# Output products of a fused attention and expert kernel: one-bank PSUM tiles instead of two-bank tiles, and a list maker that counts a matmul's restart

## The chip, the cores and the metric

One NeuronCore of one Trainium2 chip runs the whole program. The metric is device time in microseconds of one execution; lower is better. Before the change the median of three runs is 1176.81 us (1176.42 to 1177.85).

## The reference

An attention block with pooled keys feeds two feed-forward blocks. All arithmetic is float32.

```python
a = softmax(phi, axis=2)                              # per head, 576 tokens x 32 memories
k_m, v_m = a^T k, a^T v
x = softmax(q k_m^T / 8) v_m                          # -> x: 2304 tokens x 512
h = x @ w_in; x = (h * cos(h)) @ w_out                # 512 -> 2048 -> 512
p = domain_probs / (domain_probs.sum(-1) + 1e-9)      # 2304 x 4
for e in range(4):
    out += p[:, e:e+1] * (max(x @ w1[e], 0) @ w2[e])  # 512 -> 1024 -> 512 for each expert
```

## The kernel before, in words

A float32 product is made of three passes (`mm3`, L308): each operand is split into a high and a low float32r part, and high times high, high times low and low times high are added up in PSUM.

**Two stages.** The attention and the first feed-forward block end at about 377 us; they follow a written order (`PLAN`) and the change does not touch them. The second stage, the four experts, is the rest. It runs over u (two halves of the tokens), s (16 slices of 256 hidden columns, four for each expert) and j (two token groups of a half, 512 and 640 tokens). One (u, s, j) is a unit; there are 64.

**A unit** has these parts. `hidden` (L1060, task H) makes x @ w1 with seven block products in place of eight (a Strassen-like scheme), each of six matmuls, of 256 or of 320 columns, in three PSUM banks out of a ring `p` of four. Between some products ScalarE copies a partial sum out (tiles `p1`, `u2`, `u3`, names p and u in the trace), and VectorE adds them (L925, tile `c`); so the chain of a unit goes back and forth between engines. `rectify` (L1122, task R) applies the maximum with zero.

In the **first half** (u = 0), `plain_out` (L1184, task O) multiplies a tile of 128 tokens with w2: six matmuls of 512 columns fill one PSUM bank, and VectorE's `gather` (L934) scales by p and adds to `acc` (L939; L937 where s = 0, the first write). A unit has four or five such tiles, a slice nine. They are grouped in twos: a task takes one entry of the ring `po`, that is a PSUM tile `op` of two banks, and makes product, gather, product, gather in it (L1193 to L1206). There are two such entries, so four banks. The group with the fifth tile uses one of its two banks.

In the **second half** (u = 1) the output is made for pairs of token tiles by the same seven-product scheme: `pair_prep` (L1214) builds the operands and `pair_out` (L1266) makes seven products of three matmuls with 256 columns each, in one two-bank tile `op` of the ring `po`. Names in the code: px is in the first bank, pz and py share the second. px is used over and over: m1, out, m6, out, m7, out, m4, out. The first "out" (e1) goes over ScalarE (tile `ev`, L341) with an addition afterwards, the next ones (e3, e5) over VectorE's gather. Then e6 gathers px and py together (512 columns), m3 adds to py, and e7 gathers pz and py (512 columns). The tokens that are left over in a half take `plain_out` with a bank of the ring `p`.

**The order of the work** is made while the program is built, by the class `Order` (L148). Each task is a generator that yields one operation after the other; its next operation is its head. `run` (L225) looks at all heads, reckons for each when it could start (`start`, L191: when its engine is free and its dependencies have ended, by the planned durations), and puts the earliest one into the program, between equals the one with the lower rank. Ranks: H of unit i has 10 i, O of unit i has 10 i + 11 and up (u = 0) or 10 i + 13 and up (u = 1). The engines then run their lists in order. Waits between engines come from the tile framework, by what each instruction reads and writes of a tile.

```python
t = max([self.at[eng], *(d.end for d in op.deps)])            # L192
o = yield pe(1400, 130, mm, t0, done[key], done["wb", u, s])  # L1204
m1 = yield prod(px, 0, 0, t0, ...)                            # L1304
m2 = yield prod(pz, 1, 1)
e1 = yield from grown(0, da[:, 0], op[:, px], pa, m1)
m5 = yield prod(py, 3, 3)
m6 = yield prod(px, 4, 4, e1, more=True)
```

Of the kernel before, what the change touches and what calls it, by code (L numbers as in the profile page):

```python
# [9 lines left out]
F32 = mybir.dt.float32  # L10
# [7 lines left out]
PSUM = bass.MemoryType.PSUM  # L18
# [47 lines left out]
class Have:  # L66
    def __init__(self, keys):
# [64 lines left out]
FIRST = "00 01 10 11 02 12 03 13".split()  # L132
PAIRS = ((0,), (1,), (2, 3), (4, 5), (6, 7))
RINGS = dict(phi=3, kv=4, q=4, raw=2, wi=2, wf=1, wo=2, es=2, st=2, stT=1, kvs=1, vw=2, y=2, kk=1, gt=3, h=2, o=2, c=2,
             p2=2, raw2=2, tt=1, wa=2, wb=2, wt=2, cq=2, p1=1, u2=1, u3=1, ht=2, h7=4, h1=1, sm=2, p=4, po=2, ev=4)
PATIENCE = {"PE": 0.0, "ACT": 0.5, "DVE": 0.5, "POOL": 1.0, "SP": 0.5, "X": 0.0}
RK = (0, -2, 8, 13, 20)
EV, ONE_P = (0,), True
RX = (12, 305, 333)
BW, BP, BX, RL = 20.0, 1.5, 1.2, -15  # L140
HOP = 90.0
TABLE_NS = 1283.0
DMA_NS = 1.0 / 370.0
DMA_LAG = 2000.0
# [3 lines left out]
class Order:  # L148
# [3 lines left out]
    def __init__(self):  # L152
        self.at = dict.fromkeys(("PE", "ACT", "DVE", "POOL", "SP", "X"), 0.0)
        self.table, self.port, self.bus = None, 0.0, 0.0
        self.tasks = {}
        self.done = {}
        self.left = {}
        self.log = []

    def add(self, name, rank, gen):  # L160
        self.tasks[name] = [rank, gen, None, name]
# [26 lines left out]
            else:  # L188
                return

    def start(self, op, eng):  # L191
        t = max([self.at[eng], *(d.end for d in op.deps)])  # L192
        if eng == "ACT" and op.table and op.table != self.table:
            t += TABLE_NS
        return max(t, self.port) if eng in op.port else t
# [29 lines left out]
    def run(self):  # L225
        while self.tasks:
            moved = None
            while moved != (moved := [t[2] for t in self.tasks.values()]):
                for task in sorted(self.tasks.values(), key=lambda t: t[0]):
                    self.poll(task)  # L230
            heads = []
            for task in self.tasks.values():
                if isinstance(task[2], Op):
                    op = task[2]
                    engs = op.engs if op.free else op.engs[:1]
                    _, t, eng = min((self.start(op, e) + op.ns[e] * (op.free if e == "DVE" and op.free else 1.0), self.start(op, e), e)
                                    for e in engs)
# [9 lines left out]
def tile_kernel(  # L247
# [17 lines left out]
    NT, DM = out.shape  # L265
# [68 lines left out]
    def have(*keys):  # L334
        return Have(keys)
# [10 lines left out]
    def pe(ns, lat, fn, *deps, fill=None):  # L346
        return Op("PE", ns, fn, *deps, lat=lat, fill=fill)
# [560 lines left out]
    dram = ctx.enter_context(tc.tile_pool(name="dram", bufs=1, space=bass.MemoryType.DRAM))  # L908
    p_ctx.close()
    ps_p = ctx.enter_context(tc.tile_pool(name="ps_p", bufs=4, space=PSUM, reuse_waits="tile"))  # L910
    ps_q = ctx.enter_context(tc.tile_pool(name="ps_q", bufs=2, space=PSUM, reuse_waits="tile"))

    PROD = {1: (0, 0), 2: (1, 1), 3: (2, 2), 4: (6, 3), 5: (3, 4), 6: (4, 5), 7: (5, 6)}
    HD2 = DM // 2
# [42 lines left out]
        todo.count((kind, 0, s), USERS[kind], R[kind], k, o)  # L957

    NBYTES = {"wa": 128 * 4 * 2 * XOPS * 256, "wb": 128 * 4 * 2 * NFC * DM, "wt": 128 * 4 * 8 * HD2}
    USERS = {"wa": 3, "wb": 6, "wt": 1}  # L960

    def make_wa(s):
        yield have(("wa?", s - 1), ("wb?", s - 1))
# [217 lines left out]
        n = seq.setdefault(name, len(seq))  # L1181
        return ("O?", n - 1), ("O?", n)

    def plain_out(i, tts, name, at, key, free):  # L1184

        u, s, j = units[i]
        before_, mine = turn(name)
        yield have(key, ("wb", u, s), before_, ("x", 0, 1))
        ring = "p" if u and ONE_P else "po"
        ko, t0 = yield R[ring]  # L1190
        todo.set(mine, None)
        wb, kb_ = w[u * NS2 + s][1]
        if ring == "po":  # L1193
            op = ps_q.tile([128, 2, DM], F32, tag="q", name="op")
        else:
            op = ps_p.tile([128, 1, DM], F32, tag="p", name="op")
        for e, tt in enumerate(tts):
            lt = at(tt)

            def mm():  # L1200
                for fc in range(NFC):
                    mm3(op[:, e], lambda x: lt(x, fc), lambda x: wb[:, x, fc, :], fc == 0, fc == NFC - 1)

            o = yield pe(1400, 130, mm, t0, done[key], done["wb", u, s])  # L1204
            ti, p_ = share(i, tt)
            g = yield gather(DM, outv[:, ti, :], op[:, e], p_, s == 0, o, done["x", 0, 1])  # L1206
            if d := store(i, ti, g):
                yield d
        R[ring].give(ko, g)
        free(o)  # L1210
        todo.set(("done", name), None)
        todo.count(("wb", u, s), USERS["wb"] - u, R["wb"], kb_, o)

    def pair_prep(i, k):  # L1214

# [50 lines left out]
    def pair_out(i, k, name):  # L1266

        u, s, j = units[i]
        before_, mine = turn(name)
        yield have(("h7", i, k), ("wb", u, s), ("wt", u, s), before_, ("x", 0, 1))  # L1270
        ko, t0 = yield R["po"]
        todo.set(mine, None)
        (wb, kb_), (wt, kt) = w[u * NS2 + s][1:]
        ht, kh = h7s[i, k]
        b = [lambda x: wb[:, x, 0, :HD2], lambda x: wb[:, x, 1, :HD2], lambda x: wb[:, x, 1, HD2:]]
        b += [lambda x, m=m: wt[:, x, m] for m in range(4)]
        op = ps_q.tile([128, 4, HD2], F32, tag="q", name="op")
        px, pz, py = 0, 2, 3
        (ia, pa), (ib, pb) = (share(i, t) for t in tiles_of(j)[0][k])
        da, db = (outv[:, i_, :].rearrange("p (x d) -> p x d", x=2) for i_ in (ia, ib))  # L1280

        def prod(at, oa, ob, *deps, more=False):
            return pe(357, 130, lambda: mm3(op[:, at], lambda x: ht[x][:, oa], b[ob], not more, True, True), *deps)

        first = s == 0

# [14 lines left out]
        def plus(dst, t, o, kt):  # L1301
            R["ev"].give(kt, (yield two_(HD2, dst, dst, t, o, op=ALU.add)))

        m1 = yield prod(px, 0, 0, t0, done["h7", i, k], done["wb", u, s], done["wt", u, s])  # L1304
        m2 = yield prod(pz, 1, 1)
        e1 = yield from grown(0, da[:, 0], op[:, px], pa, m1)
        m5 = yield prod(py, 3, 3)
        m6 = yield prod(px, 4, 4, e1, more=True)
        e3 = yield from grown(1, da[:, 1], op[:, px], pa, m6)
        m7 = yield prod(px, 5, 5, e3, more=True)  # L1310
        e5 = yield from grown(2, db[:, 1], op[:, px], pb, m7)
        m4 = yield prod(px, 2, 6, e5, more=True)
        if first:
            e6 = yield gather(HD2, db[:, 0], op[:, px], pb, True, m4)
            e6 = yield gather(HD2, db[:, 1], op[:, py], pb, False, m5)
        else:
            e6 = yield gather(DM, db, op[:, px::py - px], pb, False, m4, m5)
        m3 = yield prod(py, 6, 2, e6, more=True)
        R["h7"].give(kh, m3)
        todo.count(("wb", u, s), USERS["wb"] - u, R["wb"], kb_, m3)  # L1320
        todo.count(("wt", u, s), 4, R["wt"], kt, m3)
        if d := store(i, ib, e6):
            yield d
        e7 = yield gather(DM, da, op[:, pz:], pa, False, m3, m2)
        R["po"].give(ko, e7)
        if d := store(i, ia, e7):
            yield d

    def swap():
# [6 lines left out]
        todo.set("swap", None)  # L1336

    with tc.manual_schedule():
        for kind in ("wa", "wb", "wt"):
            todo.set(("got?", kind, -1), None)  # L1340
        todo.set(("wa?", 1), None)
# [15 lines left out]
        for i, (u, s, j) in enumerate(units):  # L1357
            todo.add(f"H{i}", 10 * i + RK[0], hidden(i))
            nt = 2 * SUBS[j][1] // 128
            if not u:  # L1360
                groups = [list(range(t, min(t + 2, nt))) for t in range(0, nt, 2)]
                for g, tts in enumerate(groups):
                    def free(o, i=i, n_=len(groups)):
                        todo.count(("ht", i), n_, R["ht"], cs_[i][1], o)
# [3 lines left out]
                    todo.add(f"O{i}.{g}", 10 * i + 11 + g, plain_out(i, tts, f"O{i}.{g}", at, ("ht", i), free))  # L1368
                todo.add(f"R{i}", 10 * i + RK[1], rectify(i))
                continue  # L1370
            todo.add(f"R{i}", 10 * i + RK[1], rectify(i))
            def pairs(i=i):
                for k in range(2):
                    todo.add(f"P{i}.{k}", 10 * i + RK[2] + k, pair_prep(i, k))
                    todo.add(f"O{i}.{k}", 10 * i + RK[3] + k, pair_out(i, k, f"O{i}.{k}"))

            def left(i=i, j=j):
                todo.add(f"Q{i}", 10 * i + RK[2] + 2 * (i != FINAL), one_prep(i))
                for t in tiles_of(j)[1]:
                    todo.add(f"O{i}.2", 10 * i + RK[3] + 2 * (i != FINAL), plain_out(  # L1380
                        i, [t], f"O{i}.2", lambda tt: lambda x, fc: ones_[i][0][:, x, fc], ("h1", i),
                        lambda o: R["h1"].give(ones_[i][1], o)))
            for f in (left, pairs) if i == FINAL else (pairs, left):
                f()
# [55 lines left out]
```

## Time and profile before

| | |
|---|---|
| median of three runs | 1176.81 us |
| the profiled execution | 1176.0 us |
| its span, first to last instruction | 1174.2 us |
| TensorE busy (matmuls) | 1141.1 us, 97% |
| VectorE, ScalarE, GpSimd busy | 797.4, 547.6, 674.9 us |
| mean granted TensorE clock | 0.995 |

The matmuls' ends in the profile are modelled: two that follow each other overlap in their rows. So the engine's pace is read from the starts. A matmul row comes with a row of its weight load (PEld), which runs ahead under the matmul before it; where a matmul has to wait for a semaphore, its weight load waits too.

### The profile page before, as it was taken

What the parts mean: (1) busy time and instruction counts of PE and PEld (TensorE: products, weight loads), DVE (VectorE), ACT (ScalarE), POOL (GpSimd) and SP (SyncE); (2) the same over time, 40 slices, a digit from 0 to 9 for tenths busy, and PEclk for the clock granted to TensorE, in tenths of its full rate; (3) what the DMA queues carried; (4) which work ended last, traced back from release to release, by engine and by line L of the source; (5) the groups of instructions that cost most, each with busy time, mean ns of one, the idle gap of its engine ahead of it and who ended that gap; (6) DMA issues with size and microseconds to landing.
All of it is one profiled execution on the core that took longest, in us unless ns stands there. A gap on an engine that the chain in (4) does not pass through costs nothing.

```text
span 1174.2 us, 21445 instructions
## 1 busy us (share of the span) xinstructions
PE 1141.1 (97%) x8432; PEld 1053.5 (90%) x8432; DVE 797.4 (68%) x1328; ACT 547.6 (47%) x1113; POOL 674.9 (57%) x964
## 2 busy tenths in 40 slices
PE   8999999999999899999999999999999999999997
PEld 7689999999999788888888888888999999999996
DVE  5888778788777655555555555687676767676766
ACT  4886555455544333343333333344554454545552
POOL 1555243133214458667776677756777676766764
PEclk9999999999999999999999999999999999999999
DMA  8931212211103444655666556692643454335412
GB/s 301 369 94 43 86 55 73 75 53 37 37 1 144 162 152 177 254 189 189 239 256 251 195 188 224 268 363 103 242 163 135 158 199 183 135 136 222 182 73 81
DMA packets 46485, 190.43 MB, mean 162 GB/s; under 512 B 6192, under 2 KB 15408, under 8 KB 34096
## 3 DMA queue, kind: packets, MB, share of 16 engines
q1 hardware_dynamic: 46384, 189.06, 43.7%
q8 instruction: 66, 1.08, 0.4%
q14 instruction: 35, 0.29, 0.1%
HBM read 121.41 MB, written 67.63 MB: 161 GB/s over the span
## 4 chain that ended last, share of the span: by engine, by line
PE 89%; DVE 6%; DMA 2%; ACT 1%; issue 1%; SPq 0%; DVEq 0%; ACTq 0%
PE op L310 49%; PE hp L310 36%; DVE acc L939 2%; DMA q<-in_qt_dram 1%; PE vw_ps L594 1%; DVE h L355 1%; PE warm L724 1%; DMA kv<-in_kv_dram 1%; PE sc L531 1%; ACT ev L341 1%; DVE x L355 1%; PE kvp L478 0%; SPq L338 0%; DVE c L925 0%; DVE sA L355 0%
## 5 line engine op out<-in xcount | busy, mean ns | idle before, releaser
L310 PE MATMUL hp<-x,wa 128*128 128x320 f32 (+1 forms) x2688 | 406.9, 296 | 6.0 <-DVE c L925 3.5
L310 PEld LDWEIGHTS hp<-x,wa 128*128 128x128 f32 x2688 | 379.1, 188 | 19.6 <-DVE c L925 5.2
L939 DVE SCALAR_TENSOR_TENSOR acc<-op,p_all,acc 128x512 f32<-128x512 f32 (+1 forms) x402 | 260.5, 662 | 184.0 <-PE op L310 180.2
L310 PE MATMUL op<-wb,ht 128*128 128x512 f32 x864 | 225.1, 402 | 5.7 <-DVE acc L937 4.0
L310 PE MATMUL op<-gt,wo 128*128 128x288 f32 x1536 | 218.9, 296 | 0.7 <-DVE acc L698 0.6
L310 PEld LDWEIGHTS op<-gt,wo 128*128 128x128 f32 x1536 | 208.2, 188 | 6.6 <-issue 2.8
L310 PEld LDWEIGHTS op<-wb,ht 128*128 128x128 f32 x864 | 156.3, 189 | 43.1 <-DVE acc L939 9.6
L355 POOL TENSOR_TENSOR gt<-y,gt 128x576 fp32r<-128x576 f32 x41 | 60.4, 1472 | 165.3 <-ACT gt L341 142.8
L341 ACT ACTIVATE u<-hp 128x320 f32<-128x320 f32 (+1 forms) x128 | 52.6, 411 | 203.1 <-PE hp L310 203.1
L310 PE MATMUL op<-wt,h 128*128 128x256 f32 x768 | 121.9, 286 | 9.5 <-ACT ev L341 5.8
L310 PEld LDWEIGHTS op<-wt,h 128*128 128x128 f32 x768 | 104.6, 189 | 15.2 <-ACT ev L341 8.7
L355 POOL TENSOR_TENSOR sm<-c 128x128 f32<-128x128 f32 x128 | 62.3, 491 | 92.5 <-ACT c L341 92.1
L310 PE MATMUL op<-wb,h 128*128 128x256 f32 (+1 forms) x672 | 113.1, 298 | 2.1 <-DVE acc L939 2.0
L310 PE MATMUL hp<-attnT,vw 128*128 128x288 f32 x768 | 112.4, 296 | 0.5 <-POOL attnT L355 0.5
L310 PEld LDWEIGHTS hp<-attnT,vw 128*128 128x128 f32 x768 | 105.1, 188 | 3.3 <-issue 1.2
L698 DVE TENSOR_TENSOR acc<-op,acc 128x576 f32<-128x576 f32 (+1 forms) x120 | 84.4, 710 | 32.4 <-PE op L310 31.6
L310 PEld LDWEIGHTS op<-wb,h 128*128 128x128 f32 x672 | 94.4, 189 | 5.7 <-DVE acc L939 2.1
L355 POOL TENSOR_TENSOR wt<-w2m,wt 128x256 fp32r<-128x256 f32 x64 | 54.4, 872 | 76.8 <-ACT wt L341 76.8
L925 DVE TENSOR_TENSOR c<-hp,u 128x320 f32<-128x320 f32 (+1 forms) x128 | 57.8, 451 | 29.9 <-ACT u L341 16.2
L355 POOL TENSOR_TENSOR h<-c,h 128x128 fp32r<-128x128 f32 (+1 forms) x121 | 71.2, 608 | 2.6 <-ACT h L341 2.6
L928 DVE SCALAR_TENSOR_TENSOR ht<-c,ht 128x256 fp32r<-128x256 f32 (+1 forms) x64 | 56.2, 878 | 19.8 <-ACT ht L341 19.5
L341 ACT ACTIVATE p<-hp 128x256 f32<-128x256 f32 (+1 forms) x64 | 25.9, 405 | 89.7 <-PE hp L310 89.7
(118 smaller groups left out, 1466.1 us busy)
## 6 DMA issues: line engine op xcount, KB each, us to landing
wa_d<-wa SPq DMA_DIRECT2D x16, 1792.0 KB, 10.1
wa<-wa_d SPq DMA_DIRECT2D x16, 1792.0 KB, 8.6
raw<-in_w_dram SPq DMA_DIRECT2D x32, 512.0 KB, 8.7
wt_d<-wt SPq DMA_DIRECT2D x16, 1024.0 KB, 5.0
wb_d<-wb SPq DMA_DIRECT2D x16, 1024.0 KB, 9.6
wt<-wt_d SPq DMA_DIRECT2D x16, 1024.0 KB, 7.0
wb<-wb_d SPq DMA_DIRECT2D x16, 1024.0 KB, 4.9
kv<-in_kv_dram SPq DMA_DIRECT2D x16, 512.0 KB, 7.7
```

Source lines behind the costliest of these rows:

```text
L310: nc.tensor.matmul(out=ps, lhsT=lt(a), rhs=rt(b), start=first and i == 0, stop=last and i == 2, skip_group_check=more,)
L341: return Op("ACT", ns, fn or (lambda: nc.scalar.activation(out=out, in_=in_, func=func, **kw)), *deps, table=table)
L355: eng.tensor_tensor(out=out, in0=in0, in1=in1, op=op)
L531: nc.tensor.matmul(out=sc[32 * i:32 * i + 32, :TH], lhsT=kvT[b][p0:p0 + 64, 0, i, :], rhs=qt[p0:p0 + 64, i, :], start=True, stop=True,)
L594: nc.tensor.matmul(out=ps[32 * i:32 * i + 32, g, j * FS:j * FS + FS], lhsT=kvT[b][64 * g:64 * g + 64, 1, i, :], rhs=wi[s][0][64 * g:64 * g ...
L698: e = yield dve(155 + 301 * nd, lambda: nc.vector.tensor_tensor(out=dst, in0=op[:, :, :TH], in1=dst, op=ALU.add), o)
L724: nc.tensor.matmul(out=warm[:, :128], lhsT=ones, rhs=ones, start=True, stop=True)
L925: return dve(157 + 1.045 * n, lambda: nc.vector.tensor_tensor(out=out, in0=ps, in1=sb, op=ALU.add), *deps)
L928: return dve(155 + 1.05 * n, lambda: nc.vector.scalar_tensor_tensor(out=out, in0=in0, scalar=0.0, in1=f32(hi), op0=ALU.max, op1=ALU.subtra ...
L939: nc.vector.scalar_tensor_tensor(out=dst, in0=ps, scalar=pe, in1=dst, op0=ALU.mult, op1=ALU.add)
```

## The change

The ring `po` has four entries of one bank each. In the first half every tile of 128 tokens is a task of its own (nine a slice) with one bank. A pair of the second half takes two entries: a tile `bx` for px and a tile `bo` for pz and py. Its steps stand in another order: e1 before m2; py's gather e6 alone (256 columns), before m7 (where s = 0, after e5); m4, then m3 with no gather between them; then e7 (px, 256 columns) and e8 (pz and py, 512 columns). The list maker, in the second stage only, adds 160 ns to the start of a TensorE operation whose dependencies end later than 60 ns before TensorE is free, and, when it compares heads, 200 ns to the end of a TensorE operation's dependencies. The counters of the users of `wb` and `wt` follow.

```diff
-             ... sm=2, p=4, po=2, ev=4)
+             ... sm=2, p=4, po=4, ev=4)
+STALL, SLACK = 160.0, {"PE": 200.0}
...
-    def start(self, op, eng):
-        t = max([self.at[eng], *(d.end for d in op.deps)])
+    def start(self, op, eng, slack=0.0):
+        t = max([d.end for d in op.deps], default=0.0) + slack
+        if eng == "PE" and self.stall and t > self.at["PE"] - 60.0:
+            t += self.stall
+        t = max(self.at[eng], t)
...
-                    _, t, eng = min((self.start(op, e) + op.ns[e] * (...), self.start(op, e), e)
-                                    for e in engs)
+                    _, t, eng = min((self.start(op, e, self.slack.get(e, 0.0)) + op.ns[e] * (...),
+                                     self.start(op, e, self.slack.get(e, 0.0)), e) for e in engs)
...
-    ps_q = ctx.enter_context(tc.tile_pool(name="ps_q", bufs=2, space=PSUM, reuse_waits="tile"))
+    ps_q = ctx.enter_context(tc.tile_pool(name="ps_q", bufs=4, space=PSUM, reuse_waits="tile"))
...
-    USERS = {"wa": 3, "wb": 6, "wt": 1}
+    USERS = {"wa": 3, "wb": 10, "wt": 1}
...
+    def bank_of(ring):
+        return (ps_q if ring == "po" else ps_p).tile([128, DM], F32, tag="q" if ring == "po" else "p", name="op")
+
-    def plain_out(i, tts, name, at, key, free):
+    def plain_out(i, tt, name, at, key, free):
...
-        if ring == "po":
-            op = ps_q.tile([128, 2, DM], F32, tag="q", name="op")
-        else:
-            op = ps_p.tile([128, 1, DM], F32, tag="p", name="op")
-        for e, tt in enumerate(tts):
-            lt = at(tt)
-            def mm():
-                for fc in range(NFC):
-                    mm3(op[:, e], lambda x: lt(x, fc), lambda x: wb[:, x, fc, :], fc == 0, fc == NFC - 1)
-            o = yield pe(1400, 130, mm, t0, done[key], done["wb", u, s])
-            ti, p_ = share(i, tt)
-            g = yield gather(DM, outv[:, ti, :], op[:, e], p_, s == 0, o, done["x", 0, 1])
-            if d := store(i, ti, g):
-                yield d
+        op = bank_of(ring)
+        lt = at(tt)
+        def mm():
+            for fc in range(NFC):
+                mm3(op, lambda x: lt(x, fc), lambda x: wb[:, x, fc, :], fc == 0, fc == NFC - 1)
+        o = yield pe(1400, 130, mm, t0, done[key], done["wb", u, s])
+        ti, p_ = share(i, tt)
+        g = yield gather(DM, outv[:, ti, :], op, p_, s == 0, o, done["x", 0, 1])
         R[ring].give(ko, g)
+        if d := store(i, ti, g):
+            yield d
...
+        kx, tx_ = yield R["po"]
         ko, t0 = yield R["po"]
...
-        op = ps_q.tile([128, 4, HD2], F32, tag="q", name="op")
-        px, pz, py = 0, 2, 3
+        bx, bo = bank_of("po"), bank_of("po")
+        px, pz, py = bx[:, :HD2], bo[:, :HD2], bo[:, HD2:]
...
-        m1 = yield prod(px, 0, 0, t0, done["h7", i, k], done["wb", u, s], done["wt", u, s])
-        m2 = yield prod(pz, 1, 1)
-        e1 = yield from grown(0, da[:, 0], op[:, px], pa, m1)
+        m1 = yield prod(px, 0, 0, tx_, done["h7", i, k], done["wb", u, s], done["wt", u, s])
+        e1 = yield from grown(0, da[:, 0], px, pa, m1)
+        m2 = yield prod(pz, 1, 1, t0)
         m5 = yield prod(py, 3, 3)
         m6 = yield prod(px, 4, 4, e1, more=True)
-        e3 = yield from grown(1, da[:, 1], op[:, px], pa, m6)
+        e3 = yield from grown(1, da[:, 1], px, pa, m6)
+        e6 = None
+        if not first:
+            e6 = yield gather(HD2, db[:, 1], py, pb, False, m5, m2)
         m7 = yield prod(px, 5, 5, e3, more=True)
-        e5 = yield from grown(2, db[:, 1], op[:, px], pb, m7)
+        e5 = yield from grown(2, db[:, 1], px, pb, m7)
+        if first:
+            e6 = yield gather(HD2, db[:, 1], py, pb, False, m5, m2)
         m4 = yield prod(px, 2, 6, e5, more=True)
-        if first:
-            e6 = yield gather(HD2, db[:, 0], op[:, px], pb, True, m4)
-            e6 = yield gather(HD2, db[:, 1], op[:, py], pb, False, m5)
-        else:
-            e6 = yield gather(DM, db, op[:, px::py - px], pb, False, m4, m5)
         m3 = yield prod(py, 6, 2, e6, more=True)
...
-        e7 = yield gather(DM, da, op[:, pz:], pa, False, m3, m2)
-        R["po"].give(ko, e7)
+        e7 = yield gather(HD2, db[:, 0], px, pb, first, m4)
+        R["po"].give(kx, e7)
...
+        e8 = yield gather(DM, da, bo, pa, False, m3)
+        R["po"].give(ko, e8)
...
     with tc.manual_schedule():
+        todo.stall, todo.slack = STALL, SLACK
...
-                groups = [list(range(t, min(t + 2, nt))) for t in range(0, nt, 2)]
-                for g, tts in enumerate(groups):
+                for g in range(nt):
...
```

## Rows read from the trace of the kernel before

**Rows 1.** The page, section 1: busy time, share of the span, instructions of each engine.
```profile
PE 1141.1 (97%) x8432; PEld 1053.5 (90%) x8432; DVE 797.4 (68%) x1328; ACT 547.6 (47%) x1113; POOL 674.9 (57%) x964
```

**Rows 2.** Timeline of TensorE, one slice of the first half: start, duration (us), count.
```profile
563.07 4.37 PE L310 MATMUL op<-wb,ht 128*128 128x512 f32 x18
567.28 3.68 PE L310 MATMUL hp<-x,wa 128*128 128x320 f32 x24
570.80 1.56 PE L310 MATMUL op<-wb,ht 128*128 128x512 f32 x6
572.19 1.04 PE L310 MATMUL hp<-x,wa 128*128 128x320 f32 x6
573.20 1.66 PE L310 MATMUL op<-wb,ht 128*128 128x512 f32 x6
574.70 1.92 PE L310 MATMUL hp<-x,wa 128*128 128x320 f32 x12
...
586.28 1.59 PE L310 MATMUL hp<-x,wa 128*128 128x256 f32 x12
587.71 4.37 PE L310 MATMUL op<-wb,ht 128*128 128x512 f32 x18
```

**Rows 3.** Timeline of all engines around one wait of that slice.
```profile
572.39 0.75 DVE L939 SCALAR_TENSOR_TENSOR acc<-op,p_all,acc 128x512 f32<-128x512 f32 x1 [1.72 <-PE op L310]
573.20 1.23 PEld L310 LDWEIGHTS op<-wb,ht 128*128 128x128 f32 x6 [0.23 <-DVE acc L939]
```

**Rows 4.** Waits of the weight loads, 405 to 740 us: total us, times, longest.
```profile
PEld op L310 <- DVE acc L939: 9.3, 38, 0.3
```

**Rows 5.** Timeline of all engines, beginning of the second stage.
```profile
394.99 2.96 PE L310 MATMUL op<-wb,ht 128*128 128x512 f32 x12
...
400.42 0.82 DVE L355 TENSOR_TENSOR x<-sB,x 128x640 fp32r<-128x640 f32 x1 [0.80 <-ACT x L341]
401.16 0.74 DVE L937 TENSOR_SCALAR acc<-op,p_all 128x512 f32<-128x512 f32 x1
...
401.96 2.93 PE L310 MATMUL op<-wb,ht 128*128 128x512 f32 x6 [4.01 <-DVE acc L937]
...
404.69 1.48 PE L310 MATMUL hp<-x,wa 128*128 128x320 f32 x8
```

**Rows 6.** Busy by window: length, then PE, PEld, DVE, ACT, POOL; granted clock; DMA.
```profile
402.00:405.00 3.00, 3.00 (x8) 2.42 (x9) 0.07 (x1) 0.00 (x0) 2.83 (x4) 0.50 1.08 437
```

**Rows 7.** The chain that ended last: a line of each of two periods (start, length).
```profile
923.03 2.11 DVE h L355
...
970.45 2.11 DVE h L355
```

**Rows 8.** Waits of the weight loads, 800 to 1150 us: total us, times, longest.
```profile
PEld op L310 <- ACT ev L341: 8.7, 14, 0.8
PEld hp L310 <- DVE c L925: 4.7, 6, 0.8
```

**Rows 9.** Timeline of all engines, one such wait in the second half.
```profile
941.11 0.52 PE L310 MATMUL op<-wb,h 128*128 128x256 f32 x3
...
941.67 0.47 ACT L341 ACTIVATE ev<-op,p_all 128x256 f32<-128x256 f32 x1 [0.80 <-PE op L310]
...
942.20 0.98 PE L310 MATMUL op<-wt,h 128*128 128x256 f32 x6 [0.57 <-ACT ev L341]
...
943.01 0.87 PE L310 MATMUL hp<-x,wa 128*128 128x256 f32 x6
```

**Rows 10.** The end: TensorE's waits from 1150 us, and its last products.
```profile
PE op L310 <- DVE acc L939: 4.5, 7, 1.3
...
1169.46 0.92 PE L310 MATMUL op<-wb,h 128*128 128x256 f32 x3 [0.96 <-DVE acc L939]
```

**Rows 11.** VectorE's gathers, 800 to 1150 us: count, busy, mean ns, idle before.
```profile
L939 DVE SCALAR_TENSOR_TENSOR acc<-op,p_all,acc 128x512 f32<-128x512 f32 x129 | 95.4, 748 | 56.5 <-PE op L310 55.9
L939 DVE SCALAR_TENSOR_TENSOR acc<-op,p_all,acc 128x256 f32<-128x256 f32 x116 | 55.5, 479 | 28.0 <-PE op L310 28.0
```

**Rows 12.** Busy by window, ten slices of the second half (columns as in rows 6).
```profile
875.00:1112.00 237.00, 230.19 (x1742) 224.20 (x1740) 166.59 (x296) 117.15 (x311) 164.17 (x306) 1.00 0.42 167
```

More of the change, by code (lines that the diff above doesn't have):

```diff
@@ L134 @@
 RINGS = dict(phi=3, kv=4, q=4, raw=2, wi=2, wf=1, wo=2, es=2, st=2, stT=1, kvs=1, vw=2, y=2, kk=1, gt=3, h=2, o=2, c=2,
-             p2=2, raw2=2, tt=1, wa=2, wb=2, wt=2, cq=2, p1=1, u2=1, u3=1, ht=2, h7=4, h1=1, sm=2, p=4, po=2, ev=4)
+             p2=2, raw2=2, tt=1, wa=2, wb=2, wt=2, cq=2, p1=1, u2=1, u3=1, ht=2, h7=4, h1=1, sm=2, p=4, po=4, ev=4)
 PATIENCE = {"PE": 0.0, "ACT": 0.5, "DVE": 0.5, "POOL": 1.0, "SP": 0.5, "X": 0.0}
@@ L158, in __init__ @@
         self.log = []
+        self.stall, self.slack = 0.0, {}
     def add(self, name, rank, gen):
@@ L235, in run @@
                     engs = op.engs if op.free else op.engs[:1]
-                    _, t, eng = min((self.start(op, e) + op.ns[e] * (op.free if e == "DVE" and op.free else 1.0), self.start(op, e), e)
-                                    for e in engs)
+                    _, t, eng = min((self.start(op, e, self.slack.get(e, 0.0)) + op.ns[e] * (op.free if e == "DVE" and op.free else 1.0),
+                                     self.start(op, e, self.slack.get(e, 0.0)), e) for e in engs)
                     heads.append((t, task[0], eng, task))
@@ L1192, in plain_out @@
         wb, kb_ = w[u * NS2 + s][1]
-        if ring == "po":
-            op = ps_q.tile([128, 2, DM], F32, tag="q", name="op")
-        else:
-            op = ps_p.tile([128, 1, DM], F32, tag="p", name="op")
-        for e, tt in enumerate(tts):
-            lt = at(tt)
-            def mm():
-                for fc in range(NFC):
-                    mm3(op[:, e], lambda x: lt(x, fc), lambda x: wb[:, x, fc, :], fc == 0, fc == NFC - 1)
-            o = yield pe(1400, 130, mm, t0, done[key], done["wb", u, s])
-            ti, p_ = share(i, tt)
-            g = yield gather(DM, outv[:, ti, :], op[:, e], p_, s == 0, o, done["x", 0, 1])
-            if d := store(i, ti, g):
-                yield d
+        op = bank_of(ring)
[6 more added lines that the diff above has]
+        g = yield gather(DM, outv[:, ti, :], op, p_, s == 0, o, done["x", 0, 1])
         R[ring].give(ko, g)
+        if d := store(i, ti, g):
+            yield d
         free(o)
         todo.set(("done", name), None)
-        todo.count(("wb", u, s), USERS["wb"] - u, R["wb"], kb_, o)
+        todo.count(("wb", u, s), 6 - 1 if u else USERS["wb"], R["wb"], kb_, o)
     def pair_prep(i, k):
@@ L1282, in prod @@
         def prod(at, oa, ob, *deps, more=False):
-            return pe(357, 130, lambda: mm3(op[:, at], lambda x: ht[x][:, oa], b[ob], not more, True, True), *deps)
+            return pe(357, 130, lambda: mm3(at, lambda x: ht[x][:, oa], b[ob], not more, True, True), *deps)
         first = s == 0
@@ L1302, in plus @@
             R["ev"].give(kt, (yield two_(HD2, dst, dst, t, o, op=ALU.add)))
-        m1 = yield prod(px, 0, 0, t0, done["h7", i, k], done["wb", u, s], done["wt", u, s])
-        m2 = yield prod(pz, 1, 1)
-        e1 = yield from grown(0, da[:, 0], op[:, px], pa, m1)
+        m1 = yield prod(px, 0, 0, tx_, done["h7", i, k], done["wb", u, s], done["wt", u, s])
+        e1 = yield from grown(0, da[:, 0], px, pa, m1)
+        m2 = yield prod(pz, 1, 1, t0)
         m5 = yield prod(py, 3, 3)
         m6 = yield prod(px, 4, 4, e1, more=True)
-        e3 = yield from grown(1, da[:, 1], op[:, px], pa, m6)
+        e3 = yield from grown(1, da[:, 1], px, pa, m6)
+        e6 = None
+        if not first:
+            e6 = yield gather(HD2, db[:, 1], py, pb, False, m5, m2)
         m7 = yield prod(px, 5, 5, e3, more=True)
-        e5 = yield from grown(2, db[:, 1], op[:, px], pb, m7)
+        e5 = yield from grown(2, db[:, 1], px, pb, m7)
+        if first:
+            e6 = yield gather(HD2, db[:, 1], py, pb, False, m5, m2)
         m4 = yield prod(px, 2, 6, e5, more=True)
-        if first:
-            e6 = yield gather(HD2, db[:, 0], op[:, px], pb, True, m4)
-            e6 = yield gather(HD2, db[:, 1], op[:, py], pb, False, m5)
-        else:
-            e6 = yield gather(DM, db, op[:, px::py - px], pb, False, m4, m5)
         m3 = yield prod(py, 6, 2, e6, more=True)
         R["h7"].give(kh, m3)
-        todo.count(("wb", u, s), USERS["wb"] - u, R["wb"], kb_, m3)
-        todo.count(("wt", u, s), 4, R["wt"], kt, m3)
-        if d := store(i, ib, e6):
+        todo.count(("wb", u, s), 5, R["wb"], kb_, m3)
+        todo.count(("wt", u, s), 4, R["wt"], kt, m4)
+        e7 = yield gather(HD2, db[:, 0], px, pb, first, m4)
+        R["po"].give(kx, e7)
+        if d := store(i, ib, e7):
             yield d
-        e7 = yield gather(DM, da, op[:, pz:], pa, False, m3, m2)
-        R["po"].give(ko, e7)
-        if d := store(i, ia, e7):
+        e8 = yield gather(DM, da, bo, pa, False, m3)
+        R["po"].give(ko, e8)
+        if d := store(i, ia, e8):
             yield d
@@ L1360, in tile_kernel, with free @@
             if not u:
-                groups = [list(range(t, min(t + 2, nt))) for t in range(0, nt, 2)]
-                for g, tts in enumerate(groups):
-                    def free(o, i=i, n_=len(groups)):
-                        todo.count(("ht", i), n_, R["ht"], cs_[i][1], o)
+                for g in range(nt):
+                    def free(o, i=i, nt=nt):
+                        todo.count(("ht", i), nt, R["ht"], cs_[i][1], o)
                     def at(tt, i=i):
                         return lambda x, fc: cs_[i][0][:, x, fc, tt * 128:tt * 128 + 128]
-                    todo.add(f"O{i}.{g}", 10 * i + 11 + g, plain_out(i, tts, f"O{i}.{g}", at, ("ht", i), free))
+                    todo.add(f"O{i}.{g}", 10 * i + 11 + g, plain_out(i, g, f"O{i}.{g}", at, ("ht", i), free))
                 todo.add(f"R{i}", 10 * i + RK[1], rectify(i))
@@ L1380, in left @@
                     todo.add(f"O{i}.2", 10 * i + RK[3] + 2 * (i != FINAL), plain_out(
-                        i, [t], f"O{i}.2", lambda tt: lambda x, fc: ones_[i][0][:, x, fc], ("h1", i),
+                        i, t, f"O{i}.2", lambda tt: lambda x, fc: ones_[i][0][:, x, fc], ("h1", i),
                         lambda o: R["h1"].give(ones_[i][1], o)))
```

## The prediction

> **What bounds the kernel now.** The page comes first: TensorE is busy 97% of the span, every other engine at most 68% [rows 1]. The 97% does not say that nothing is left, because the rows of matmuls that follow each other overlap; the pace has to be read from starts. So the second view is TensorE's timeline of one slice of the first half [rows 2]. Eighteen products of 512 columns take 567.28 - 563.07 = 4.21 us, 0.234 each; 24 of 320 columns take 3.52 us, 0.147 each; 12 of 256 columns take 1.43 us, 0.119 each. A slice holds 54, 42 and 42 of them: 12.63 + 6.16 + 5.01 = 23.80 us without any wait. It lasts 587.71 - 563.07 = 24.64 us, so 0.84 us is lost inside a "busy" engine.
>
> Where, the same rows say. Six products of 320 columns start at 572.19 and should end at 573.07; the next start at 573.20, and these six then take 1.50 us where six at pace take 1.40. So a wait costs its length and about 0.10 us of restart. The third view, all engines around that point, names the cause [rows 3]: the weight load stands still until VectorE's gather ends (572.39 + 0.75 = 573.14). That gather began 0.2 us after the tile of 570.80 to 572.19 was finished: it reads the other bank of the same two-bank tile. The second product of a task waits for the gather of the first, though they share no bank.
>
> The fourth view counts: 38 such waits between 405 and 740 us [rows 4], three a slice, so 12.7 slices, and 12.7 x 0.84 = 10.6 us.
>
> The second half is read the same way. Two slices take 970.45 - 923.03 = 47.42 us [rows 7]; their products at pace (84 of 320, 84 + 168 of 256 and 12 of 512 columns: 12.35 + 29.99 + 2.81) take 45.15 us. 2.27 us is lost in two slices. Two waits carry it [rows 8]: 14 for ScalarE's copy `ev`, 6 of the hidden products for a sum on VectorE. A wait of the first kind [rows 9]: three products start at 941.11 and should end at 941.47; the copy runs from 941.67 to 942.14; the next products start at 942.20. These are m5 and m6. m6 adds to px, which the copy reads, and has to wait; m5 writes py, in the other bank, and waits for the tile alone. Besides, the copy e1 stands behind m2 in the list although it only needs m1.
>
> **The change, part by part**, against the profiled execution's own 1176.0 us, which is 0.8 us under the median of the runs.
>
> *One bank a tile, first half.* A product now needs only the gather four tiles earlier. Four tiles of 1.40 us are 5.6 us of products, a gather is 0.75 us, and VectorE has begun each within 0.2 us of its product where nothing else was queued [rows 3]: that wait ends last nowhere. The 38 waits are worth 10.6 us at most and nothing at least (if the list maker uses the freedom to burn tiles early, and hidden products then wait instead). I take 9.5, near the upper end, because all of them have the one cause that goes. Next late would be the hidden products behind ScalarE's copies; the single tiles are what covers them, and their number is the same.
>
> *Beginning of the stage.* Two tiles start at 394.99, then TensorE waits until 401.96 for the first gather, which itself waits for the operand x [rows 5]. [...] With four free banks the four tiles of the first unit run on to 394.99 + 5.6 = 400.6; x is ready at 401.24, and the hidden products that start at 404.69 now can start at about 401.35, with four tiles done instead of three: 3.34 + 1.40 = 4.7 us at most. I take 4, since the list may still put a gather between the tiles (then 0).
>
> *Pairs with two tiles, e1 ahead of m2.* m5 no longer waits for e1, and e1 starts one product (0.36 us) earlier. The 14 waits hold 8.7 us of still weight loads [rows 8], and the one shown lost 0.73 us between products where the weight load stood for 0.77 [rows 8, 9]; by that share 8.2 us, with 14 restarts of 0.10 us 9.6 us. Between nothing and 9.6 I take 8.5: the wait that remains, m6 on e1, has m2 and m5 (0.72 us) ahead of it now.
>
> *The list maker's margin.* Nothing in the tiles frees the 6 hidden products that wait for VectorE's sum (4.7 us and 6 restarts, 5.3 us). Another product with margin may be put ahead: between 0 and 5.3, I take 1.7, a third, since the rank still puts hidden products first.
>
> *m3 without a gather before it.* It counts where no other product is left, at the end: seven waits of 4.5 us, the last of 0.96 us ahead of m3 [rows 10]. That last one goes, with its restart, and part of the others: between 0 and 4.5, I take 2.
>
> *More gathers.* A pair outside s = 0 gathers 256 columns twice where it gathered 512 at once: 2 x 479 - 748 = 210 ns more [rows 11], for 60 pairs 12.6 us of VectorE, 0.84 us a slice. VectorE is idle 237.00 - 166.59 = 70 us in ten slices [rows 12], 7 us a slice; that covers it, and I put nothing on the path. With the cover gone it would cost up to 12.6 us.
>
> *New waits* that the new order makes: ten restarts, 1 us.
>
> Sum: 9.5 + 4 + 8.5 + 1.7 + 2 - 1 = 24.7 us; 1176.0 - 24.7 = 1151.3, so 1151 us.
>
> **Rivals.** *The waits move.* VectorE and ScalarE answer no faster than before; what stood behind a shared tile stands behind the copy it really needs. For it: six waits in the second half are real dependencies already. Against it: in the first half not one of the listed waits is. Then half of the two large terms is left (4.75 + 4.25) and the beginning (4), nothing else: 1163 us.
>
> *The waits are not the tile's.* If the framework already told the banks apart, or the list maker put the same order, nothing moves: 1176 us. Against it: the gather of 572.39 reads a bank that the waiting product does not write.
>
> *Slower: py's gather in the way.* e6 now stands on VectorE between e3 and e5, in a pair's serial chain. If a pair's product m7 is listed with nothing ready beside it, e5 ends up to 0.48 us later and TensorE restarts, 0.58 us for each of 60 pairs: 35 us. With the terms of the first half gained (13.5) and nothing in the second that is 1176 + 21 = 1197 us. The point: m7 takes 0.36 us and its hand-over 0.2, so e6 (0.48 us, started with m7) is over before e5 is due; it decides only where VectorE has a queue by then, and it is idle 30% of the time.
>
> *Slower: the clock falls.* In these rows short waits never cost clock: through ten slices of the second half, with their waits, it is 1.00 [rows 12], and the one 0.50 in the stage follows a pause of 4 us [rows 5, 6]. Were it to fall once in each of 32 slices for the 3 us of rows 6, each would lose 2.73 - 1.40 = 1.33 us on six products, about 1.46 us in 3.00, 47 us in all, against 24.7 gained: 1198 us. [...]
>
> **How the numbers follow.** Forecast 0.70; waits that move 0.20; no effect 0.05; the gather in the way 0.04; the clock 0.01. With all terms at their best (10.6 + 4.7 + 9.6 + 5.3 + 4.5 = 34.7) the time is 1141; at the other end I take in the rival at 1163 and a little of the gathers' cost: 1165. Below 0.2% (2.4 us) a measurement of this kernel can hardly tell a change from none. Faster by more 0.90, within it 0.05, slower 0.05.
>
> **What would show it.** Right: a slice of the first half near 23.8 us, two of the second near 45.5; no wait of a product of `wb` and `ht` on L939 between 405 and 740 us; no 0.50 in the clock near 402 us and the idle stretch there under 1 us; `ev` gone from TensorE's waits; more gathers of 256 columns by 120, fewer of 512 by 60. Wrong: hidden products waiting for ScalarE's copies three times a slice, or a queue on VectorE ahead of e5.

## The result and the profile after

The changed kernel takes 1139.68 us (median of four runs, 1138.49 to 1141.34) against 1176.84 us (four runs too): 0.9684 of the time, 95% interval 0.9667 to 0.9701, so 37.2 us less. The forecast was 1151, its range 1141 to 1165. The sign and the main mechanism held; the gain is half as large again as the sum, and the time lies just under the range. The step that failed is named in the section on the prediction.

The page after, section 1 (compare [rows 1]):

```profile
PE 1120.5 (98%) x8432; PEld 1047.3 (92%) x8432; DVE 796.4 (70%) x1385; ACT 546.8 (48%) x1113; POOL 682.5 (60%) x967
```

VectorE has 57 instructions more and is busy no longer. Where the time came from is read by cutting both second stages at the same three points: the start of the first hidden product with 320 columns, of the first hidden product of the second half, and of the last hidden product. Busy time by window, before (window, length, then PE, PEld, DVE, ACT, POOL, granted clock, DMA):

```profile
377.28:404.69 27.41, 21.82 (x141) 19.32 (x140) 18.45 (x28) 10.71 (x21) 15.73 (x16) 0.94 0.33 110
404.69:775.83 371.14, 369.50 (x2077) 324.70 (x2076) 206.74 (x324) 135.51 (x259) 257.52 (x332) 1.00 0.60 221
775.83:1152.97 377.14, 365.62 (x2736) 354.69 (x2735) 265.39 (x475) 184.13 (x485) 257.24 (x469) 1.00 0.43 167
1152.97:1174.22 21.25, 12.88 (x81) 10.57 (x79) 12.01 (x22) 3.67 (x10) 7.98 (x15) 0.89 0.29 112
```

The same after:

```profile
377.43:401.69 24.26, 21.94 (x146) 19.68 (x145) 17.65 (x29) 10.68 (x21) 11.84 (x12) 1.00 0.26 89
401.69:759.50 357.81, 357.81 (x2072) 321.57 (x2071) 204.50 (x326) 135.62 (x259) 258.94 (x334) 1.00 0.64 236
759.50:1120.98 361.48, 359.26 (x2739) 352.75 (x2738) 266.88 (x527) 184.07 (x486) 268.13 (x476) 1.00 0.46 174
1120.98:1138.47 17.49, 11.11 (x78) 9.62 (x76) 12.55 (x26) 3.20 (x9) 7.23 (x14) 0.94 0.36 136
```

Beginning and first half together fall from 398.55 to 382.07 us, 16.5 us (they are taken together because one tile more now stands ahead of the first cut). The second half gives 15.7, the end 3.8. The three parts are 35.9 us; the first stage is 0.15 us later in this execution, which leaves the 35.7 us between the two spans. In the first half the engine is busy for all of its 357.81 us.

TensorE's timeline of a slice after (compare [rows 2]):

```profile
577.09 4.37 PE L315 MATMUL op<-wb,ht 128*128 128x512 f32 x18
581.30 3.68 PE L315 MATMUL hp<-x,wa 128*128 128x320 f32 x24
584.82 1.56 PE L315 MATMUL op<-wb,ht 128*128 128x512 f32 x6
586.22 1.05 PE L315 MATMUL hp<-x,wa 128*128 128x320 f32 x6
587.10 1.55 PE L315 MATMUL op<-wb,ht 128*128 128x512 f32 x6
588.49 1.92 PE L315 MATMUL hp<-x,wa 128*128 128x320 f32 x12
...
600.87 4.37 PE L315 MATMUL op<-wb,ht 128*128 128x512 f32 x18
```

600.87 - 577.09 = 23.78 us a slice, the pace without waits that the prediction counted (23.80). The tile at 587.10 starts 0.88 us after six products of 320 columns, and takes 1.39 us: no wait and no restart. The beginning of the stage after (compare [rows 5, 6]), and its clock:

```profile
396.08 5.77 PE L315 MATMUL op<-wb,ht 128*128 128x512 f32 x24
401.69 3.68 PE L315 MATMUL hp<-x,wa 128*128 128x320 f32 x24
```

```profile
400.00:405.00 5.00, 5.00 (x31) 4.64 (x31) 3.87 (x7) 1.69 (x3) 2.92 (x4) 1.00 1.02 427
```

Four tiles run through and the hidden products follow without a pause; the granted clock stays at 1.00. The chain that ended last shows a slice's period in the second half (compare [rows 7]):

```profile
905.84 3.54 PE op L315 x24
...
928.38 3.54 PE op L315 x24
...
950.93 3.54 PE op L315 x24
```

Two slices take 45.09 us instead of 47.42. What TensorE still waits for in the whole second stage (total us, times, longest):

```profile
PE hp L315 <- ACT u L346: 2.5, 5, 0.5
PE op L315 <- DVE acc L944: 2.4, 3, 1.2
PE op L315 <- DVE acc L942: 1.3, 2, 0.7
PE hp L315 <- ACT p L346: 0.8, 1, 0.8
```

These are all the waits that the view lists there. Neither `ev` nor the sum `c` is among them; what is left lies at the beginning, between the halves and at the end. VectorE's gathers from 377 us on: 512 columns, before 274, and 256 columns, before 128 of them:

```profile
L944 DVE SCALAR_TENSOR_TENSOR acc<-op,p_all,acc 128x512 f32<-128x512 f32 x214 | 159.3, 746 | 96.1 <-PE op L315 95.7
L944 DVE SCALAR_TENSOR_TENSOR acc<-op,p_all,acc 128x256 f32<-128x256 f32 x248 | 113.3, 477 | 39.5 <-PE op L315 36.4
```

### The profile page after: what moved, and what is told of

The parts are those of the page before. It is cut to its first block, busy times and chain, and to the rows that moved or that the text cites. A ratio compares the mean times of both kernels' runs of the same rounds, so it can differ in the third digit from the quotient of the medians.

```text
span 1138.5 us, 21515 instructions
## 1 busy us (share of the span) xinstructions
PE 1120.5 (98%) x8432; PEld 1047.3 (92%) x8432; DVE 796.4 (70%) x1385; ACT 546.8 (48%) x1113; POOL 682.5 (60%) x967
## 4 chain that ended last, share of the span: by engine, by line
PE 93%; DMA 3%; DVE 2%; ACT 1%; issue 0%; SPq 0%; DVEq 0%; ACTq 0%
PE op L315 50%; PE hp L315 39%; PE vw_ps L599 1%; DMA kv<-in_kv_dram 1%; DMA q<-in_qt_dram 1%; PE warm L729 1%; DMA phi<-in_phi_dram 1%; DVE acc L944 1%; PE sc L536 0%; PE kvp L483 0%; DVE acc L703 0%; DMA raw<-in_w_out_dram 0%; DVE sA L360 0%; DVE y L653 0%; DVE h L360 0%
## 5 line engine op out<-in xcount | busy, mean ns | idle before, releaser
L315 PE MATMUL hp<-x,wa 128*128 128x320 f32 (+1 forms) x2688 | 401.0, 296 | 3.3 <-ACT u L346 2.5
L944 DVE SCALAR_TENSOR_TENSOR acc<-op,p_all,acc 128x512 f32<-128x512 f32 (+1 forms) x462 | 264.3, 602 | 135.6 <-PE op L315 132.1
L315 PE MATMUL op<-wb,ht 128*128 128x512 f32 x864 | 216.8, 395 | 0.0
L315 PE MATMUL op<-wt,h 128*128 128x256 f32 x768 | 125.1, 282 | 3.6 <-DVE acc L944 2.4
L315 PE MATMUL op<-wb,h 128*128 128x256 f32 (+1 forms) x672 | 122.6, 297 | 0.0
L315 PEld LDWEIGHTS op<-wb,h 128*128 128x128 f32 x672 | 98.8, 188 | 3.1
L360 POOL TENSOR_TENSOR wt<-w2m,wt 128x256 fp32r<-128x256 f32 x64 | 47.3, 761 | 67.7 <-ACT wt L346 67.7
L360 POOL TENSOR_TENSOR h<-c,h 128x256 fp32r<-128x256 f32 (+1 forms) x127 | 76.4, 622 | 1.1 <-ACT h L346 1.1
L360 POOL TENSOR_TENSOR wb<-raw,wb 128x256 fp32r<-128x256 f32 x64 | 56.6, 911 | 29.7 <-ACT wb L346 28.8
```

What stands on the lines that cost most here:

```text
L315: nc.tensor.matmul(out=ps, lhsT=lt(a), rhs=rt(b), start=first and i == 0, stop=last and i == 2, skip_group_check=more,)
L360: eng.tensor_tensor(out=out, in0=in0, in1=in1, op=op)
L944: nc.vector.scalar_tensor_tensor(out=dst, in0=ps, scalar=pe, in1=dst, op0=ALU.mult, op1=ALU.add)
```

## The experiments

All are compared with runs of the kernel before on the same chip, whose median there was 1171.6 to 1177.4 us. "Stretches" are the lengths of beginning and first half together, second half and end, cut at the three points above; before they are 398.6, 377.1 and 21.3 us, after the change 382.1, 361.5 and 17.5. Small differences are read from the stretches rather than from whole times: after the first stage, which no edit touches, the first hidden product starts anywhere from 374.7 to 379.7 us in these executions, while the change and its repeat e9 have the same three stretches to 0.1 us. On the chip of e9 and e10 the kernel before is some 5 us faster than in the result above and the changed kernel is not, so ratios are compared on one chip only.

| run | us | ratio (95% interval) | stretches, us |
|---|---|---|---|
| e1 one-bank tiles in the first half, order as before | 1157.73 | 0.9844 (0.9828 to 0.9860) | 381.2, 375.4, 21.0 |
| e2 all but the list maker's rules | 1142.80 | 0.9714 (0.9696 to 0.9731) | 381.1, 364.1, 19.2 |
| e3 the list maker's rules alone | 1185.17 | 1.0077 (1.0062 to 1.0092) | 402.7, 382.2, 21.6 |
| e4 the change with the old steps of a pair | 1143.64 | 0.9726 (0.9710 to 0.9743) | 382.1, 366.5, 17.7 |
| e5 = e3, the list maker told of the tile's waits | 1144.96 | 0.9726 (0.9700 to 0.9751) | 383.9, 363.5, 19.1 |
| e6 tiles alone: old steps, old rules | 1142.33 | 0.9706 (0.9684 to 0.9728) | 381.1, 363.8, 19.9 |
| e7 the change, restart counted, no margin | 1140.92 | 0.9694 (0.9673 to 0.9715) | 381.5, 363.3, 18.7 |
| e8 the change, margin, restart not counted | 1139.12 | 0.9680 (0.9657 to 0.9702) | 381.1, 361.4, 18.1 |
| e9 the change again, beside e10 | 1139.53 | 0.9731 (0.9716 to 0.9746) | 382.1, 361.5, 17.5 |
| e10 the change with two more edits | 1137.64 | 0.9706 (0.9693 to 0.9719) | 381.2, 361.0, 17.6 |
| e11 before, told of the tile's waits, old rules | 1153.28 | 0.9798 (0.9782 to 0.9814) | 386.0, 369.3, 19.3 |

**e1: is the wait the shared tile's?** The instructions of each engine and their order are those of before.

```diff
-            op = ps_q.tile([128, 2, DM], F32, tag="q", name="op")
+            op = [ps_q.tile([128, DM], F32, tag="q", name="op") for _ in tts]
```

Expected: 

> The kernel before, with one edit: in the first half a task's two output products get a tile of one bank each instead of one tile of two banks. The order of the work on every engine is that of before; pairs keep their two-bank tile. Theory A (the wait is the shared tile's, so that alone carries the first half): the 38 waits for L939 between 405 and 740 us go, 10.6 us, and of the pause near 398 us the third tile no longer waits, 3.3 us or more: about 1163 us. Theory B (the list maker's new order did it; the tile only took part): the order is that of before, so the waits stay or move to the hidden products: 1172 us or more.

Measured: 18.2 us less, more than the 10.6 + 3.3 = 13.9 us of theory A. Between 405 and 740 us no wait for the gather is left, and beginning and first half give 17.4 us, all that the change gives there and 0.9 more. The traces list the same operations in the same order on every engine as before, so the waits were the tile's. The pairs' waits are still there: 14 for `ev`, as before, and 6 for the sum `c`, where the kernel before has 8 from 377 us on:

```profile
PEld op L310 <- ACT ev L341: 8.6, 14, 0.8
PEld hp L310 <- DVE c L927: 3.5, 6, 0.8
```

**e2: without the list maker's rules.**

```diff
     with tc.manual_schedule():
-        todo.stall, todo.slack = STALL, SLACK
```

Expected: 

> The changed kernel with the list maker of before (no restart counted, no margin): tiles of one bank, single tasks, pairs' new steps. Theory A: all but the waits that no tile frees is gained, about 1145 us. Theory B: freed tiles alone let the list maker fill the gaps with work that is ready in the plan at the last moment, and restarts of 0.1 to 0.3 us come up everywhere: 1152 us or more.

Measured: 1142.8 us, on theory A's side and 2 us better than it. The rules are worth about 3 us of the 37 (runs on different chips): 2.6 us in the second half (364.1 against 361.5) and 1.7 at the end, less 1.0 that they cost at the beginning.

**e3: the list maker's rules alone.** The two hunks of `start` and `run` and the line that switches them on, on the kernel before.

Expected: 

> The kernel before with the new list maker only; all tiles, tasks and steps of a pair as before. Theory A: the list maker does not know of the wait inside a tile, so the three waits a slice of the first half stay and only some of the second half's go: 1166 to 1176 us. Theory B: it does most of the work: 1155 us or less.

Measured: slower, 1.0077, which neither theory had; A had only said that the waits would stay. The waits for `ev` rise from 14 to 26 (800 to 1150 us; compare [rows 8]):

```profile
PEld op L315 <- ACT ev L346: 18.2, 26, 0.8
PEld op L315 <- DVE acc L942: 0.7, 2, 0.4
```

One of them in the timeline:

```profile
944.18 0.52 PE L315 MATMUL op<-wb,h 128*128 128x256 f32 x3
...
944.73 0.47 ACT L346 ACTIVATE ev<-op,p_all 128x256 f32<-128x256 f32 x1 [0.79 <-PE op L315]
...
945.26 0.62 PE L315 MATMUL op<-wt,h 128*128 128x256 f32 x3 [0.56 <-ACT ev L346]
...
945.72 0.39 PE L315 MATMUL hp<-x,wa 128*128 128x256 f32 x2
```

Three products alone start at 945.26: it is m5 without m6. In the list maker's account m5 depends on nothing, so no margin and no restart hold it back, and it is put right behind m2; on the chip it stands there until the copy ends, and hidden products that have nothing to do with it queue behind it. If that is the reason, telling the list maker must turn the sign: e5. It is not the whole loss: of the 9.5 us that the stretches lose, 4.1 lie in beginning and first half, where the granted clock is 0.52 on average from 400 to 407 us and the two-bank tile's waits are those of before (39 in 405 to 740 us). The waits of the hidden products for the sum `c` are as good as gone here too, though the tiles and the steps are those of before (weight loads from 377 us on):

```profile
PEld hp L315 <- DVE c L930: 0.2, 1, 0.2
```

**e5: the same, told of the waits that the tile makes.** The two-bank tiles stay.

```diff
-            o = yield pe(1400, 130, mm, t0, done[key], done["wb", u, s])
+            o = yield pe(1400, 130, mm, t0, done[key], done["wb", u, s], g)
...
-        e1 = yield from grown(0, da[:, 0], op[:, px], pa, m1)
-        m5 = yield prod(py, 3, 3)
+        e1 = yield from grown(0, da[:, 0], op[:, px], pa, m2)
+        m5 = yield prod(py, 3, 3, e1)
```

(g is the gather of the task's first product.) Expected: 

> The list maker alone (as in e3) on the kernel before, but told of the waits that the two-bank tile makes: the second product of a task depends on the first one's gather, m5 on e1, e1 on m2. Theory A (e3 lost because the list maker counts on products as ready that the tile holds back): it now puts other work there, so the time falls well below e3's 1185 us, to 1160 to 1172. Theory B (the margin itself does harm while there are two entries in the ring): 1180 us or more.

Measured: 1144.96 us, 15 us under theory A's own range. With not one tile split, 32 of the 37 us are there; the weight loads' waits from 800 to 1150 us are down to:

```profile
PEld op L315 <- DVE acc L944: 3.0, 7, 1.0
PEld op L315 <- issue: 2.3, 2, 1.2
```

**e11: told, with the old rules.** As e5 without the line that switches restart and margin on.

Expected: 

> The kernel before with one thing told to its old list maker (no restart, no margin): the waits that the two-bank tile makes (second product on the first one's gather, m5 on e1, e1 on m2). If it is the list maker's blindness that cost the time, and not the shared tile: 1144 to 1152 us. If the restart and the margin are what turned e3 into e5: 1165 us or more.

Measured: 1153.28 us, 1.3 us above the range given to blindness alone and far from 1165. So the told dependencies alone are worth about 23 us, restart and margin 8 more where the tile still holds products back (on one-bank tiles, e2 against the change, 3). The waits from 800 to 1150 us are now nearly all for gathers:

```profile
PEld op L315 <- DVE acc L944: 8.8, 19, 1.1
PEld op L315 <- issue: 0.3, 1, 0.3
```

**e4 and e6: the steps of a pair.** Both have m1 and m2 ahead of e1, and e6 after m4; e6 has the old rules besides.

```diff
-        e1 = yield from grown(0, da[:, 0], px, pa, m1)
-        m2 = yield prod(pz, 1, 1, t0)
+        m2 = yield prod(pz, 1, 1)
+        e1 = yield from grown(0, da[:, 0], px, pa, m1)
...
         m4 = yield prod(px, 2, 6, e5, more=True)
+        e7 = yield gather(HD2, db[:, 0], px, pb, first, m4)
+        e6 = yield gather(HD2, db[:, 1], py, pb, False, m5, m2)
         m3 = yield prod(py, 6, 2, e6, more=True)
```

Expected of e4: 

> The changed kernel with a pair's steps in the old order (m1 and m2 before e1; py gathered only after m4, so m3 waits for it again), still with two tiles. Theory A (the two tiles free m5, the order is worth little outside the end): 1140 to 1143 us. Theory C (e1 behind m2 and m3 behind a gather were the second half's waits): 1146 us or more, with waits of m6 for the copy or of m3 for a gather in every slice.

Expected of e6: 

> The changed kernel with the old list maker and a pair's old steps: one-bank tiles and single tasks alone. Theory A (the tiles carry nearly all, steps and list maker a rest each): 1144 to 1149 us, the waits for the copy of m6's px and of the hidden products still there in the second half. Theory C (without the steps the freed tiles are worth little in the second half): 1152 us or more.

Measured: e4 1143.64 us, between its two theories: 4 us worse than the change. Its second half is 5.0 us longer, but not by m6 or m3; the weight loads of hidden products wait for ScalarE's copy `u`, 18 times from 377 us on (after the change 5 times, in e6 four times):

```profile
PEld hp L315 <- ACT u L346: 7.7, 18, 0.7
PEld op L315 <- DVE acc L944: 3.4, 8, 0.7
```

e6 at 1142.33 us is 2 us under its theory A and no slower than e2, which has the new steps: without the rules the steps are worth nothing in the second half (363.8 against 364.1) and 0.7 us at the end. So steps and rules are not terms to be added: each of them alone gives about nothing or less on top of the tiles, both together 2.6 us. Why the rules on the old steps make the hidden products wait was not followed further. In e6 the waits of the hidden products for the sum `c` are down to the line below, with the old rules and the old steps. They are as short in e3, e5 and e11 (one or two, 0.2 us each), whose pairs keep the two-bank tile. So neither the tiles nor the margin is needed to remove them; what all these runs share is an order that is not that of before:

```profile
PEld hp L315 <- DVE c L930: 0.5, 2, 0.2
```

**e7 and e8: restart or margin?** The change with one of the two.

```diff
-        todo.stall, todo.slack = STALL, SLACK
+        todo.stall = STALL          # e7
+        todo.slack = SLACK          # e8
```

Expected of e7: 

> The changed kernel, restart counted (160 ns), no margin. If the restart's price is what took the last waits of the second half: 1139 to 1141 us. If the margin did: like e2, 1142 to 1143.5 us.

Expected of e8: 

> The changed kernel, margin of 200 ns, restart not counted. If the margin is what took the last waits of the second half: 1139 to 1141 us. If the restart's price did: 1142 to 1143.5 us.

Measured: e8 has the changed kernel's time and its second half (361.4 us); e7 has 363.3 us there, nearer to e2's. So the margin does it in the second half. The whole times alone would not say so: e7's lies in the range that it was given for the restart, e8's in the one for the margin, and their intervals overlap; the stretch is what tells them apart.

**e9 and e10: the rules later, and a copy over ScalarE.** The rules begin with the third unit, and where s = 0 the first copy of a pair goes over ScalarE into `acc`.

```diff
+        if i == 2:
+            todo.stall, todo.slack = STALL, SLACK
...
+            if first and e in EV:
+                return (yield act(470, dst, ps, ACTF.Copy, m, scale=p_))
```

Expected of e9: 

> The changed kernel itself, on the chip of the next run, to be compared with it: 1139 to 1141 us.

Expected of e10: 

> The changed kernel with two edits: the list maker's new rules begin with the third unit (in the first two, where no filler is ready, the margin made a wait of 0.93 us for the tile p), and where s = 0 the first copy of a pair goes over ScalarE straight into acc (two waits for L942, 1.6 us). If both waits go: 1.5 to 2.5 us faster than the changed kernel, about 1138 us. If they only move: the same time.

Measured on one chip: 1137.64 us (1136.15 to 1138.40) against 1139.53 (1138.71 to 1142.26), 1.9 us, with no run of the one above a run of the other, though the intervals of the two ratios to before overlap; by the stretches it is 1.3 us. The wait for `p` went, 0.8 us; one of the two for L942 went and the other became one for the new copy:

```profile
PEld op L315 <- ACT acc L346: 0.8, 1, 0.8
```

## Where the prediction was right, and which step of it failed

*One bank a tile, first half; beginning.* Right in kind: the waits went, the pause of 4 us went, the clock stayed at 1.00, and e1 shows that the tile alone does it. Taken were 9.5 + 4 = 13.5 us, measured 16.5. The beginning gave 27.41 - 24.26 + 1.40 = 4.6 us (1.40 for the tile that now stands ahead of the cut), the first half 371.14 - 357.81 - 1.40 = 11.9, more than the 10.6 that were held to be the most. The tenth kept back for hidden products that would wait in their place was not needed, and the first half has two more such waits than the 38 listed, 0.6 us at 0.28 each (weight loads before, 404.69 to 775.83 us); the other 0.7 us have no row.

```profile
PEld op L310 <- DVE acc L939: 9.6, 39, 0.3
PEld op L310 <- DVE acc L937: 0.2, 1, 0.2
```

*Pairs with two tiles, and the margin.* Here the sum was furthest off: 8.5 + 1.7 taken, 15.7 measured. The copy's 14 waits went as forecast. The step that failed is "Nothing in the tiles frees the 6 hidden products that wait for VectorE's sum", and with it the third of 5.3 us that was taken for them as the margin's: they went altogether, and without the margin (e2, e6, e11), even with the pairs' tiles as before (e3, e5, e11). The wait was read as the hidden chain's own. The trace before shows it as a place in VectorE's list:

```profile
922.95 2.19 DVE L355 TENSOR_TENSOR h<-c,h 128x256 fp32r<-128x256 f32 x1
925.06 0.74 DVE L939 SCALAR_TENSOR_TENSOR acc<-op,p_all,acc 128x512 f32<-128x512 f32 x1
925.72 0.41 DVE L925 TENSOR_TENSOR c<-hp,u 128x256 f32<-128x256 f32 x1
...
926.18 0.42 PEld L310 LDWEIGHTS hp<-x,wa 128*128 128x128 f32 x3 [0.79 <-DVE c L925]
```

VectorE has no pause in these rows: the sum stands behind one addition for a pair's operands (`h`) of 2.19 us. There are six such long additions before, one ahead of each of the six waits, and four in e1, which has four of these waits. In every other run the longest of them is 1.46 us, and no such wait above 0.2 us is left. Why an addition takes 2.19 us there, and 0.48 on average in e4, is not shown. The rest, 15.7 - 9.6 - 5.3 = 0.8 us, has no listed row. The pace would have told it: eight times the prediction's 45.15 us for two slices are 361.2 us, and the second half measures 361.5. This 0.8 us and the first half's 1.3 above its most are why the best end of the sum, 1141, was not low enough.

No run splits the pairs' tiles with the order held, as e1 does for the first half. So for the second half it is shown that a new order is enough (e5, e11), not what the split alone would give.

*m3 without a gather.* 2 taken, 3.8 measured at the end, inside the bounds of 0 to 4.5, but not for the reason given: in e4, where m3 stands behind a gather again, the end is 17.7 us against 17.5. That this term came near is luck. *More gathers.* At nothing, as forecast: VectorE is busy 266.9 us in the second half, 265.4 before, for 52 instructions more. *New waits.* 1 us taken, 0.8 found, in one place: the wait for `p` at the beginning, which takes both rules together (e3, e4 and e5 have it; e2, e7, e8 and e10 are without it).

*The rivals.* None came. Py's gather is not in the way: the second half runs at the counted pace. The clock did not fall: from 401.69 to 1120.98 us it is 1.00, with the banks now used one after the other. The first half after the change is no test of what short pauses do to it, because no pause is left there; the kernel before is nearer to one, and with its 40 short waits from 404.69 to 775.83 us the clock was 1.00 too. The 2.73 us of that rival are 404.69 - 401.96 in [rows 5]. Its "one 0.50 in the stage" is not the only one: at the end of the kernel before the grant is 0.59 from 1169.5 and 0.50 from 1170.0 us, behind the wait of 0.96 us of [rows 10], and the three products there last 0.92 us in the rows, against 0.52 at 941.11 [rows 9].

*What the prediction did not ask.* It took the shared tile for the cause and the list maker for a trifle. Experiments e3, e5 and e11 say it better: the wait for a shared tile exists because of the tile, and it cost time because the order was made without knowing of it. Told, the list maker finds other work: no such wait is left from 405 to 740 us and none for `ev`, and 19 for gathers stay in the second half with the old rules (e11), 7 with the new (e5).

## What to carry to other kernels

Where the order of the work is made by a program from declared dependencies, compare the waits in the trace with those it was told: a product that waits for something it does not name is a dependency that the framework adds, and it can be removed (a tile for each bank) or declared, for nearly the same gain here. Do that before refining the scheduler's costs: the same rules cost 0.8% on the undeclared waits, and gave 0.3% once the waits were gone. When the gain is a sum of many short waits, count them over the whole stretch, and let the best end of the range go down to the pace without any wait. Before a wait is called a real dependency, look at what its releaser was doing ahead of it: here it stood behind a long operation that another order puts elsewhere.

## What the runs showed of the hardware beyond that

TensorE ran this mix for 357.81 us without one pause: 1.39 to 1.40 us for six products of 512 columns, in the four tiles in a row from 396.08 us, of which none is gathered before 401.55, as in the three from 577.09, where VectorE gathers one bank while the next is written. Before the change the six products at 573.20, behind a gap of 0.13 us, took 1.50 us [rows 2], and so did the six at 579.44 and at 584.78; after it the six at 587.10, which no wait holds back, took 1.39 us. A pause of 4.0 us at the beginning went with a grant of 0.50 for the next 3.0 us [rows 5, 6]. After the change the longest pauses of the second stage are 0.93 and 1.21 us, at the end, and no row up to 1136 us, past the last product, has a lower grant behind them.
